# Retention followed by a squared-ReLU layer on one Trainium2 core: narrow idle matmuls, seven half-size products for one more block, and zeroing moved to GpSimd

## The chip, the cores and the metric

The kernel runs on one core of a Trainium2 chip. The metric is the device time of one execution in microseconds (us). Three runs of the kernel before took 204.18, 204.24 and 204.94 us; their median is 204.24 us. Engines are named as in the profile: PE is the matmul engine (PEld its weight load), DVE the vector engine, ACT the scalar engine, POOL is GpSimd, SP issues most DMAs.

## The reference, cut to what matters

```python
# q, k, v: (B=4, H=8, S=768, D=64) float32; w_in (512, 2048), w_out (2048, 512)
gamma = 1.0 - 2.0 ** (-5.0 - np.arange(H))
for t in range(S):
    state = gamma[None, :, None, None] * state + einsum('bhd,bhe->bhde', k[:, :, t], v[:, :, t])
    y[:, :, t] = einsum('bhd,bhde->bhe', q[:, :, t], state) / sqrt(D)
x = y.transpose(0, 2, 1, 3).reshape(B * S, H * D)      # 3072 tokens x 512
h = maximum(x @ w_in, 0)
out = (h * h) @ w_out                                   # 3072 x 512, float32
```

A recurrent attention ("retention") with a fixed decay for each head gives 512 numbers per token; a feed-forward layer of width 2048 with a squared ReLU follows.

## The kernel before, in words

**Tiling.** The 3072 tokens are 24 chunks of 128. The chunks are grouped in 11 blocks (`BLOCKS`, L18): block 0 has four chunks, blocks 1 to 10 have two each. For each chunk the retention is computed in its chunked form: scale q and k by powers of the decay (DVE, L361, L697), transpose them (PE, or a DMA transpose from chunk 8 on), scores (PE, L430 or L727), mask (DVE, L437 or L734), running state (PE, L458, L469 or L754, copied out to `s_bd`), outputs (PE, L498/L506 or L776/L783, copied to `xt` by ACT). For each block the layer follows: **first products** `x @ w_in` (PE, L826) into a PSUM tile, ReLU by ACT (L835), square on DVE (L806) or, for some tiles, on ACT (L804); then **second products** with `w_out`.

**Two forms of the second products.** The plain form (L1152) takes, for a chunk of 128 tokens, 16 matmuls of 128x512; a block of two chunks needs 32. In the other form (`seven_products`, L840) the product of a 2x2 partition of h (two chunks by even and odd 128-row slices) with a 2x2 partition of `w_out` is made by seven products of half the width instead of eight: 7 x 8 matmuls of 128x256 (L860), with sums of h tiles made ahead on DVE (`s1` to `s4`, L856), sums of weight tiles made once (`sum_w_out`, L319) and the results put together by DVE adds (`u`, `v`, `osb`). `SEVEN` (L28) says which blocks use it: 2 to 10. Its last product is kept (`kept`) and issued between the next block's first products. Blocks up to 2 issue their first products in units of 16 matmuls of 128x128 (`first_unit`), one for each quarter g and chunk c; later blocks in tiles of 128x512. Block 0 (`last_of_first`, L959) makes chunks 0 and 1 plainly (L1017) and chunks 2 and 3 by seven products (L984).

**What sets the order.** All instructions are issued in an order written by hand, one queue per engine, each in order; waits are semaphores. The layer's work is cut in pieces (8 for a chunk, numbered from the start), and `put(n, what, ...)` hangs attention work, loads, casts and zeroing behind piece n. `attend` (L1258) places the unpacked attention of chunks 4 to 7, `attend2` that of chunks 8 to 23. Work hung behind one piece is issued in the order in which it was put. Squares are issued at the next piece, after what is hung there.

**Buffers that matter here.** PSUM: `tp`, `st`, `y` and `c_ps` have one buffer each, `psf` four. A tile that takes a buffer waits until the last reader of the tile before it is done. `st` holds scores until DVE has masked them; `tp` holds transposes, and from block 2 on also the product `pa` of `seven_products`. In SBUF `h2` has three buffers of 128x4096 bf16, taken in turn; the first is `spare` (L1180), which lends room to block 0's `s1`, `s2`, `s4`. From block 2 on these sums lie in `k_bds` and `v_bds[0]`, which the attention of chunks 0 to 7 no longer needs.

**The start.** While q, k and v are loaded, `keep_awake` (L337) issues matmuls whose results nobody reads: 15 of 128x512, with the identity matrix as both operands, which POOL builds first.

**Zeroing.** Five tiles need zeros off their diagonal before chunk 8: `zero_off_diagonal` (L357) does it by ten DVE memsets behind pieces 35 to 44. `pack_constants` (L261) builds the decay table and the mask for chunks 8 and later; its POOL part hangs behind piece 27, its DVE and ACT part behind piece 34.

The pieces of block 0 are 5 to 32, of block 1 33 to 48. The wait in block 0 that the change touches lies in these lines: the ACT copy reads `pa`, and the next matmuls add to `pa`.

```python
nc.scalar.activation(a[:], pa, AF.Copy)          # L1041
...
product(pa, a12, b(1, 0), lo, False)             # L1047
product(pa, a12, b(1, 0), hi, False)
```

Of the kernel before, what the change touches and what calls it, by code (L numbers as in the profile page):

```python
# [9 lines left out]
FP32 = mybir.dt.float32  # L10
BF16 = mybir.dt.bfloat16
# [13 lines left out]
PACK_FROM = 8  # L25


SEVEN = range(2, 11)  # L28


@with_exitstack
def kernel(
# [148 lines left out]
        load_w_in(g)  # L181


    lng = const.tile([P, H], FP32)
    for h in range(H):
        nc.gpsimd.memset(lng[:, h : h + 1], float(np.log(gammas[h])))
# [147 lines left out]

    idle_ps = []

    def keep_awake(n, width=4 * C, pool=ps_f, name="psf"):  # L337
        if not idle_ps:
            idle_ps.append(pool.tile([P, 4, P], FP32, name=name))
        wide = max(1, width // C)  # L340
        for _ in range(n):
            nc.tensor.matmul(
                idle_ps[0][:, 0:wide, 0 : width // wide],
                lhsT=ident[:],
                rhs=ident[:, None, 0 : width // wide].to_broadcast([P, wide, width // wide]),
                start=True,
                stop=True,
            )

    def end_awake():  # L350
        idle_ps.clear()
# [3 lines left out]
    xts = {}  # L355

    def zero_off_diagonal(t, hh):  # L357
        nc.vector.memset(t[halves[hh], :, 1 - hh, :], 0.0)

    def scale(engine, out, by, table):  # L360
        engine.tensor_tensor(  # L361
# [478 lines left out]
    def seven_products(tb):  # L840
# [4 lines left out]
            t.rearrange("s p hh d -> s (p hh d)").rearrange("s (j t) -> s j t", t=C)  # L845
            for t in (k_bds[0], k_bds[1], v_bds[0])
        )
        s3 = a21
        t1, t2, t3, t4 = sums
        b11, b21, b22 = (  # L850
# [108 lines left out]
    def last_of_first():  # L959
# [43 lines left out]
        def second_products():  # L1003
            ops = [ps_f.tile([P, DM], FP32, name="psf") for _ in range(2)]
            pa, pe, pd, pb = (
                t[:, n * HN : (n + 1) * HN]
                for t in [ps_f.tile([P, DM], FP32, name="psf") for _ in range(2)]
                for n in range(2)
            )
            oa, ob = (opool.tile([P, DM], FP32, name="osb") for _ in range(2))  # L1010
            a, u, v = (upool.tile([P, HN], FP32, name=f"u{i}") for i in range(3))
            r0 = 2 * C

            def plain(j):
                for f in (2 * j, 2 * j + 1):
                    for c, op in enumerate(ops):
                        nc.tensor.matmul(  # L1017
                            op[:],
                            lhsT=h_of(0, f)[:, 0, c * C : (c + 1) * C],
                            rhs=w_out_bf[f // FPQ][:, f % FPQ, :],  # L1020
                            start=(f == 0),
                            stop=(f == NFB - 1),
                        )
                product(pa, a11, b(0, 0), (j,))

            lo, hi = range(0, 4), range(4, 8)
            for j in range(4):
                plain(j)
                yield
            product(pd, s1, t1, lo)  # L1030
            product(pb, s2, t2, lo, False)
            yield
            for j in range(4, 6):
                plain(j)
                yield
            product(pe, a22, t4, lo, False)
            yield
            plain(6)
            yield
            plain(7)  # L1040
            nc.scalar.activation(a[:], pa, AF.Copy)  # L1041
            for c, op in enumerate(ops):
                osb = opool.tile([P, DM], FP32, name="osb")
                nc.scalar.activation(osb[:], op[:], AF.Copy)
                nc.sync.dma_start(out[c * C : (c + 1) * C], osb[:])
            yield
            product(pa, a12, b(1, 0), lo, False)  # L1047
            product(pa, a12, b(1, 0), hi, False)
            nc.scalar.activation(oa[:, 0:HN], pa, AF.Copy)
            yield  # L1050
            product(pd, s1, t1, hi)
            yield
            product(pb, s2, t2, hi)
            add(u[:], pb, a[:])
            yield
            product(pe, a22, t4, hi)
            yield
            product(pb, s3, t3, lo, False)
            yield
            product(pb, s3, t3, hi, False)  # L1060
            add(v[:], pb, a[:])
            add(ob[:, HN:DM], pd, v[:])
            add(ob[:, 0:HN], pe, v[:])

            def last_product():
                product(pd, s4, b(1, 1), range(8), False)
                add(oa[:, HN:DM], pd, u[:])
                yield
                nc.sync.dma_start(out[r0 + C : r0 + 2 * C], ob[:])
                yield  # L1070
                nc.sync.dma_start(out[r0 : r0 + C], oa[:])
                yield

            kept.append(last_product())
            yield
# [5 lines left out]
    def first_unit(tb, g, c, parts=(0, 1)):  # L1081

        if tb not in h2s:
            h_tiles(tb)
        if (tb, g, c) not in open_ps:
            open_ps[tb, g, c] = ps_f.tile([P, FPQ, C], FP32, name="psf")
        hp = open_ps[tb, g, c]
        cols = slice(c * C, (c + 1) * C)
        half = FPQ // 2
        for part in parts:  # L1090
            for fq in range(part * half, (part + 1) * half):
                first_product(tb, hp[:, fq, :], g * FPQ + fq, cols)
        if 1 in parts:
            relu(h_of(tb, g * FPQ, (g + 1) * FPQ)[:, :, cols], open_ps.pop((tb, g, c)))

    def ffn_pieces(tb):
        nch = BLOCKS[tb]
# [29 lines left out]
        else:  # L1127
# [4 lines left out]
            for f0 in range(0, NFB, per):  # L1132
                hp = ps_f.tile([P, per, TB], FP32, name="psf")
                for f in range(f0, f0 + per):
                    first_product(tb, hp[:, f - f0, :], f, slice(0, TB))
                relu(h_of(tb, f0, f0 + per), hp, tb in SEVEN and f0 // per in (1, 3))
                if f0 // per in (1, 2, 3) and kept:
                    next(kept[0])
                if f0 // per == 4:
                    kept.clear()  # L1140
                if f0 // per == 5 and tb in SEVEN:
                    first_sums(slice(0, 4))
                yield
# [33 lines left out]
    def small_pt():  # L1177
        return ptpool.tile([P, NPAIR, 2, C], BF16, name="pt").rearrange("s p hh t -> s (p hh t)")

    spare = hpool.tile([P, 4096], BF16, name="h2")  # L1180
    keep_awake(7, pool=ps_y, name="y")
    scale_q4(0, 0)
    scale_q4(0, 1)
    transpose_q4(0, 0, *tp)
# [73 lines left out]
    def attend(m, scaled, places):  # L1258
        if m % 2 == 0:
            put(scaled, scale_q, m, 0)  # L1260
            put(scaled + 2 if m == 4 else scaled, scale_q, m, 1)
            put(places[0], transpose_q, m)
        put(18 if m == 4 else places[0], scale_kv, m)
        put(places[1], transpose_k, m)
        put(places[2], scores, m, 0)
        put(places[3], scores, m, 1)
        put(places[3], state, m)
        put(places[4], outputs, m)

    def attend2(m, d, before, q_at, qturn_at, k_at, turn_at, v_at):  # L1270
# [24 lines left out]
            put(place, next, made)  # L1295
    attend(4, 13, (19, 21, 23, 25, 29))
    attend(5, None, (25, 28, 30, 32, 34))
    attend(6, 31, (33, 35, 37, 39, 42))
    attend(7, None, (38, 42, 44, 46, 49))
    packed = pack_constants()  # L1300
    put(27, next, packed)
    put(34, next, packed)
    for j, t in enumerate([s_bds[2]] + ks_bd2s + v_bd2s):
        for hh in range(2):
            put(35 + 2 * j + hh, zero_off_diagonal, t, hh)
# [68 lines left out]
```

## Time and profile before

The profile is of one execution, which took 204.98 us; from its first to its last instruction it took 203.1 us.

| | |
|---|---|
| median of three runs | 204.24 us |
| profiled execution, its own time | 204.98 us |
| its span | 203.1 us |
| PE busy | 195.3 us (96%), 2351 matmuls |
| DVE busy | 154.7 us (76%) |
| ACT busy | 127.5 us (63%) |
| POOL busy | 67.5 us (33%) |

"Busy" counts from an instruction's start to its modelled end; the matmuls of one engine overlap, so how long a row of them takes is read from the start of one group to the start of the next. A bracket in a timeline, such as [1.06 <-ACT h L835], says how long the engine had been idle and which instruction's end let it go on. `x8` means that eight equal instructions are merged in one line.

### The profile page before, as it was taken

How to read it: one execution, taken by the hardware profiler on the slowest of the kernel's cores; microseconds unless marked ns; L12 is line 12 of the kernel's file. 1: busy time of each engine (PE TensorE's matmuls, PEld its weight loads, DVE VectorE, ACT ScalarE, POOL GpSimd, SP SyncE). 2: the span in 40 equal slices, each digit the busy share in tenths (PEclk: the TensorE clock that was granted, in tenths of full speed). 3: DMA queues.
4: the chain of work that ended last, by engine and by line, in shares of the span. 5: the costliest groups of instructions: out<-in, count | busy, mean ns of one | idle time of the engine just before them, and what ended most of it. 6: DMA issues, size and time to landing. Idle time of an engine off the chain costs nothing.

```text
span 203.1 us, 5810 instructions
## 1 busy us (share of the span) xinstructions
PE 195.3 (96%) x2351; PEld 162.2 (80%) x2351; DVE 154.7 (76%) x322; ACT 127.5 (63%) x258; POOL 67.5 (33%) x131
## 2 busy tenths in 40 slices
PE   5799999999999999999999999999999999999993
PEld 1368545679965998988989999999989899999883
DVE  3886798888798678788798798798797797485374
ACT  8774873365743766782794784784785775763730
POOL 8594630261300451372234325252225225100000
PEclk9999999999999999999999999999999999999999
DMA  5999999999869898989787978968899342200202
GB/s 171 353 371 398 317 192 196 249 233 263 245 164 197 213 169 141 218 221 237 148 223 137 255 219 201 255 137 208 223 151 211 114 103 58 103 3 0 107 0 103
DMA packets 92250, 38.12 MB, mean 188 GB/s; under 512 B 68544, under 2 KB 88256, under 8 KB 92224
## 3 DMA queue, kind: packets, MB, share of 16 engines
q1 hardware_dynamic: 90112, 35.66, 72.4%
q0 software_dynamic: 2112, 2.10, 6.4%
q8 instruction: 18, 0.29, 0.6%
q14 instruction: 8, 0.07, 0.1%
HBM read 27.26 MB, written 6.29 MB: 165 GB/s over the span
## 4 chain that ended last, share of the span: by engine, by line
PE 88%; DVE 4%; DMA 3%; ACT 2%; SPq 1%; issue 1%; DVEq 0%
PE psf L826 40%; PE psf L860 18%; PE tp L860 7%; PE psf L1017 3%; PE psf L1152 3%; DMA kn<-in_k_dram 3%; PE psf L984 3%; PE y L783 2%; PE st L727 2%; PE y L776 2%; PE c_ps L754 2%; DVE h L806 1%; PE c_ps L627 1%; PE y L506 1%; PE st L430 1%
## 5 line engine op out<-in xcount | busy, mean ns | idle before, releaser
L826 PE MATMUL psf<-xt,w_in_bf 128*128 128x256 bf16 (+2 forms) x880 | 92.3, 259 | 0.4 <-issue 0.4
L826 PEld LDWEIGHTS <-w_in_bf 128*128 128x128 bf16 x880 | 71.2, 98 | 11.6 <-issue 0.4
L835 ACT ACTIVATE h<-psf 128x512 bf16<-128x512 f32 x96 | 56.1, 595 | 21.5 <-PE psf L826 20.0
L806 DVE TENSOR_TENSOR h<-h 128x512 bf16<-128x512 bf16 x80 | 35.3, 455 | 18.4 <-ACT h L835 18.2
L688 POOL CAST ks_bdp<-stage 64x512 bf16<-64x512 f32 x32 | 22.7, 711 | 38.4 <-issue 34.1
L705 POOL COPY v_bd<-v 64x512 bf16<-64x512 bf16 x32 | 20.5, 642 | 44.4 <-DVE v L697 33.6
L860 PEld LDWEIGHTS <-h 128*128 128x128 bf16 x288 | 26.3, 98 | 3.6 <-DVE h L806 0.7
L860 PE MATMUL tp<-w_out_bf,h 128*128 128x256 bf16 x136 | 19.4, 273 | 0.2 <-DVE h L806 0.2
L860 PE MATMUL psf<-w_sum,h 128*128 128x256 bf16 x136 | 19.1, 273 | 0.0
L860 PE MATMUL psf<-w_sum,k_bd 128*128 128x256 bf16 x144 | 17.9, 273 | 0.0
L361 DVE TENSOR_TENSOR qs<-qn,qf 128x512 bf16<-128x512 f32 x20 | 16.2, 814 | 0.0
L860 PEld LDWEIGHTS <-k_bd 128*128 128x128 bf16 x144 | 13.7, 98 | 1.5
L856 DVE TENSOR_TENSOR osb<-psf,u 128x256 f32<-128x256 f32 x26 | 10.3, 420 | 6.1 <-PE psf L860 5.8
L763 ACT ACTIVATE s_bd<-c_ps 64x256 bf16<-64x256 f32 x29 | 10.7, 370 | 6.3 <-PE c_ps L754 6.3
L856 DVE TENSOR_TENSOR u<-psf,u 128x256 f32<-128x256 f32 x18 | 7.6, 422 | 9.3 <-PE psf L860 9.1
L697 DVE TENSOR_TENSOR v<-stage,kf 128x512 bf16<-128x512 f32 x16 | 12.1, 759 | 0.0
L734 DVE TENSOR_TENSOR pt<-st,cmask 128x512 bf16<-128x512 f32 x16 | 11.0, 687 | 0.3 <-issue 0.2
L764 ACT ACTIVATE s_bd<-c_ps 64x256 bf16<-64x256 f32 x29 | 11.0, 378 | 0.4
L856 DVE TENSOR_TENSOR k_bd<-h 128x512 bf16<-128x512 bf16 x18 | 10.7, 596 | 0.3
L790 ACT ACTIVATE xt<-y 128x512 bf16<-128x512 f32 x16 | 9.6, 598 | 1.8 <-PE y L783 1.2
L896 ACT ACTIVATE osb<-tp 128x256 f32<-128x256 f32 x8 | 3.1, 384 | 12.2 <-PE tp L860 12.2
L804 ACT ACTIVATE h<-h 128x512 bf16<-128x512 bf16 x16 | 10.1, 629 | 0.5
(145 smaller groups left out, 283.8 us busy)
## 6 DMA issues: line engine op xcount, KB each, us to landing
qn<-in_q_dram SPq DMA_DIRECT2D x12, 512.0 KB, 5.2
out_dram<-osb SPq DMA_DIRECT2D x23, 256.0 KB, 2.7
stage<-in_k_dram SPq DMA_DIRECT2D x32, 96.0 KB, 3.8
stage<-in_v_dram SPq DMA_DIRECT2D x32, 96.0 KB, 3.5
stage<-in_moe_w_in_dram SPq DMA_DIRECT2D x4, 512.0 KB, 7.2
stage<-in_moe_w_in_dram SPq DMA_DIRECT2D x2, 1024.0 KB, 10.3
w_out_bf<-in_moe_w_out_dram POOLq DMA_DIRECT2D x4, 512.0 KB, 10.2
kn<-in_k_dram SPq DMA_DIRECT2D x6, 256.0 KB, 6.3
```

What stands on the lines that cost most here:

```text
L361: engine.tensor_tensor(out=out, in0=by, in1=table[:, :, None].to_broadcast([P, H, D]), op=ALU.mult)
L688: nc.gpsimd.tensor_copy(ks[rows, :, hh, :].rearrange("s (u p) d -> s u p d", u=2), kn[rows])
L697: nc.vector.tensor_tensor(out=v2.rearrange("s (u p) d -> s u p d", u=2), in0=vn, in1=kf2[:, i, :, :, None].to_broadcast([P, 2, NPAIR, D]), ...
L705: nc.gpsimd.tensor_copy(v_bd[rows, :, hh, :], v2[rows])
L734: nc.vector.tensor_tensor(out=pt[:], in0=st[:], in1=cmask2.rearrange("s r t -> s (r t)")[:, None, :].to_broadcast([P, 2 * NPAIR, C // 2]), ...
L763: nc.scalar.activation(s_bd[halves[0], :, 0, :], c[halves[0]], AF.Copy)
L764: nc.scalar.activation(s_bd[halves[1], :, 1, :], c[halves[1]], AF.Copy)
L806: nc.vector.tensor_mul(hv, hv, hv)
L826: nc.tensor.matmul(hp, lhsT=w_in_bf[g][:, cb, fq * 128 : (fq + 1) * 128], rhs=xts[tb][:, cb, cols], start=(cb == 0), stop=(cb == NCB - 1),)
L835: nc.scalar.activation(hv, hp[:], AF.Relu)
L856: nc.vector.tensor_tensor(out=out, in0=in0, in1=in1, op=op)
L860: nc.tensor.matmul(to, lhsT=left[:, j], rhs=right(j) if callable(right) else right[:, j], start=(start and j == 0), stop=(stop and j == NF ...
```

## The change

- `keep_awake`: each idle matmul of 128x512 becomes four of 128x128. Operands are 128 columns of zeros at the end of `spare`, set by a DVE memset that is now DVE's first instruction, instead of the identity; the first batch is 10 x 4 instead of 7.
- Block 0, after the plain products: the second halves of the products `pd` and `pb` now come before the two halves of `pa += a12 * b`, which they followed.
- Block 1 joins `SEVEN`: 56 matmuls of 128x256 take the place of 32 of 128x512. Its `s1`, `s2`, `s4` lie in a further `h2` buffer (`room`), since `k_bds` and `v_bds` are still in use. One of its squares, that of unit (1, 2), goes to ACT.
- The transposed k of chunk 7 goes through `st` instead of `tp`, since `pa` of block 1 now holds `tp`.
- Both copies of chunk 6's state go to ACT; the second half of q of chunk 6 is scaled two pieces after the first, and both earlier (29, 31 instead of 31, 31); chunk 7's steps come one or two pieces earlier.
- `pack_constants` moves from pieces 27 and 34 to 18 and 22.
- The ten zeroing memsets go to POOL.
- Block 4 gets one more square on ACT (tile 6).

```diff
-SEVEN = range(2, 11)
+SEVEN = range(1, 11)
...
+    spare = hpool.tile([P, 4096], BF16, name="h2")
+    still = spare[:, 4096 - P : 4096]
+    nc.vector.memset(still, 0.0)
...
-    def keep_awake(n, width=4 * C, pool=ps_f, name="psf"):
+    def keep_awake(n, pool=ps_f, name="psf"):
...
+        for _ in range(4 * n):
+            nc.tensor.matmul(idle_ps[0][:], lhsT=still, rhs=still, start=True, stop=True)
...
     def zero_off_diagonal(t, hh):
-        nc.vector.memset(t[halves[hh], :, 1 - hh, :], 0.0)
+        nc.gpsimd.memset(t[halves[hh], :, 1 - hh, :], 0.0)
...
+        if tb == 1:
+            room = hpool.tile([P, 4096], BF16, name="h2").rearrange("e (n j t) -> e n j t", n=4, t=C)
+            s1, s2, s4 = (room[:, n] for n in range(3))
...
+            product(pd, s1, t1, hi)
+            product(pb, s2, t2, hi)
+            add(u[:], pb, a[:])
+            yield
             product(pa, a12, b(1, 0), lo, False)
+            yield
             product(pa, a12, b(1, 0), hi, False)
             nc.scalar.activation(oa[:, 0:HN], pa, AF.Copy)
-            yield
-            product(pd, s1, t1, hi)
-            yield
-            product(pb, s2, t2, hi)
-            add(u[:], pb, a[:])
             yield
...
-            relu(h_of(tb, g * FPQ, (g + 1) * FPQ)[:, :, cols], open_ps.pop((tb, g, c)))
+            relu(h_of(tb, g * FPQ, (g + 1) * FPQ)[:, :, cols], open_ps.pop((tb, g, c)), (tb, c, g) == (1, 1, 2))
...
-                relu(h_of(tb, f0, f0 + per), hp, tb in SEVEN and f0 // per in (1, 3))
+                relu(h_of(tb, f0, f0 + per), hp, tb in SEVEN and f0 // per in ((1, 3, 6) if tb == 4 else (1, 3)))
...
-    spare = hpool.tile([P, 4096], BF16, name="h2")
-    keep_awake(7, pool=ps_y, name="y")
+    keep_awake(10, pool=ps_y, name="y")
...
-            put(scaled + 2 if m == 4 else scaled, scale_q, m, 1)
+            put(scaled + 2, scale_q, m, 1)
...
-        put(places[1], transpose_k, m)
+        put(places[1], transpose_k, m, *((ps_st, "st") if m == 7 else (ps_tp, "tp")))
...
-        put(places[3], state, m)
+        put(places[3], state, m, 2 if m == 6 else 1)
...
-    attend(6, 31, (33, 35, 37, 39, 42))
-    attend(7, None, (38, 42, 44, 46, 49))
+    attend(6, 29, (33, 35, 37, 39, 42))
+    attend(7, None, (36, 40, 43, 45, 48))
     packed = pack_constants()
-    put(27, next, packed)
-    put(34, next, packed)
+    put(18, next, packed)
+    put(22, next, packed)
```

More of the change, by code (lines that the diff above doesn't have):

```diff
@@ L335 @@
     idle_ps = []
-    def keep_awake(n, width=4 * C, pool=ps_f, name="psf"):
+    def keep_awake(n, pool=ps_f, name="psf"):
         if not idle_ps:
[L339 to L348, printed above, removed]
+            idle_ps.append(pool.tile([P, P], FP32, name=name))
+        for _ in range(4 * n):
+            nc.tensor.matmul(idle_ps[0][:], lhsT=still, rhs=still, start=True, stop=True)
     def end_awake():
```

## The prediction, as it was put on record

> **What bounds the kernel.** First the page: the busy shares, then the 40 slices.
>
> ```profile
> PE 195.3 (96%) x2351; PEld 162.2 (80%) x2351; DVE 154.7 (76%) x322; ACT 127.5 (63%) x258; POOL 67.5 (33%) x131
> ...
> PE   5799999999999999999999999999999999999993
> ...
> PE 88%; DVE 4%; DMA 3%; ACT 2%; SPq 1%; issue 1%; DVEq 0%
> ```
>
> PE is full from the third slice (about 10 us) to the last; the chain that ended last is 88% PE. So a matmul taken out between 12 and 195 us shortens the kernel, and so does a PE wait that goes; work on DVE, ACT or POOL counts only where PE waits for it. I therefore looked in the timelines for starts of PE groups later than the matmuls before them allow.
>
> The first place is the end of block 0's plain products. Columns: start, duration, engine, line, operation, count, idle time and its releaser.
>
> ```profile
> 42.20 0.27 PE L984 MATMUL psf<-w_out_bf,h 128*128 128x256 bf16 x1
> 42.95 1.03 PE L984 MATMUL psf<-w_out_bf,h 128*128 128x256 bf16 x8 [0.47 <-ACT u L1041]
> ```
>
> A 256-column matmul occupies PE for 0.11 us (eight of L860 start at 76.98, the next group at 77.85), so PE was free at 42.31 and stood until 42.95: **0.64 us** for ACT's copy of `pa`.
>
> The second is block 1's second product, and what comes just before it.
>
> ```profile
> 56.09 0.39 PE L430 MATMUL st<-qT,k_bd 128*128 128x128 bf16 x4
> 56.41 0.32 PE L469 MATMUL c_ps<-v_bd,ks 128*64 128x64 bf16 x8
> 56.66 1.07 PE L826 MATMUL psf<-xt,w_in_bf 128*128 128x128 bf16 x16
> 57.56 1.89 PE L1152 MATMUL psf<-w_out_bf,h 128*128 128x512 bf16 x8
> 59.29 0.77 PE L506 MATMUL y<-pt,v_bd 128*128 128x128 bf16 x8
> ```
>
> Eight L1152 take 59.29 - 57.56 = 1.73 us.
>
> The third is DVE in the same stretch; spacings between starts are what I use below.
>
> ```profile
> 54.62 0.42 DVE L806 TENSOR_TENSOR h<-h 128x512 bf16<-128x512 bf16 x1 [1.06 <-ACT h L835]
> 54.96 0.68 DVE L437 TENSOR_TENSOR pt<-st,cmask 128x512 bf16<-128x512 f32 x1
> 55.64 0.27 DVE L358 MEMSET ks_bdp<- 64x256 uint32 x1
> 55.83 0.84 DVE L361 TENSOR_TENSOR qs<-qn,qf 128x512 bf16<-128x512 f32 x1
> 56.60 0.41 DVE L806 TENSOR_TENSOR h<-h 128x512 bf16<-128x512 bf16 x1
> 56.94 0.68 DVE L361 TENSOR_TENSOR ks<-kn,kf 128x512 bf16<-128x512 f32 x1
> 57.70 0.27 DVE L358 MEMSET ks_bdp<- 64x256 uint32 x1
> 57.99 0.69 DVE L361 TENSOR_TENSOR qs<-qn,qf 128x512 bf16<-128x512 f32 x1
> 58.60 0.42 DVE L806 TENSOR_TENSOR h<-h 128x512 bf16<-128x512 bf16 x1
> 58.93 0.69 DVE L437 TENSOR_TENSOR pt<-st,cmask 128x512 bf16<-128x512 f32 x1
> ```
>
> The mask of chunk 6's second half of scores (`pt`, 58.93) ends at 59.62, 3.3 us after its scores: DVE is behind, and in the kernel before nobody on PE asks for it until 61.84.
>
> **The change part by part.**
>
> *Wait in block 0: -0.64.* At 42.31 PE now has 8 matmuls of `pd` and `pb`, 0.87 us, ready; ACT's copy (42.51 to 42.89) ends beneath them. Their weight sums `t1`, `t2` are done by 41.5 (42.1 if shifted as in the next step).
>
> *What is late next there: +0.2.* `pack_constants` puts a cast and a multiply on DVE ahead of block 0's last sums. They need POOL's iotas, which follow the v cast (35.78, 1.10 long) by 1.0 us (41.93 lng, 42.40 iota, 0.58 long): ready at 37.9, where DVE was free at 37.4. Cast and multiply take 0.5 to 0.8 (51.24 to 52.01 before), so the sums move by 1.1 to 1.4; 0.74 of that is DVE's idle time before the mask at 39.50. What is left, 0.3 to 0.6, moves k of chunk 5 (42.61, ends 43.30) to 43.6-43.9 and `t4`'s second half (ends 44.54) to 44.9-45.1. PE, now earlier, wants them at 43.62 (42.31 + 12 x 0.109) and 44.95. I take 0.2; bounds 0 and 0.35. Without the move nothing would be late.
>
> *Second product of block 1: -0.83.* Out: 4 x 1.73 = 6.92 us. In: 7 x 0.87 = 6.09 us.
>
> *What is late next there: +0.66.* The transposes of chunk 7's k now write `st`, right behind the last unit of first products. `st` is free when DVE has masked chunk 6's second scores, the last DVE line above. PE is 0.64 - 0.2 = 0.44 us earlier, so the unit ends at 57.56 - 0.44 = 57.12. DVE's stretch starts with a square that waited for ACT, whose ReLU follows PE, so it moves with PE: 54.62 - 0.44 = 54.18. Then, by spacings and without memsets and with `ks` moved ahead into the 1.06 us of idle time: square 0.34, mask 0.61, q 0.61, square 0.34, q 0.61, square 0.34, and the mask's 0.69: 54.18 + 3.54 = 57.72, and some 0.06 to PE (`pt` 46.44 + 0.69, PE on at 47.19). So PE stands from 57.12 to 57.78: 0.66. Everything behind waits: k copies on ACT, all seven products. Bounds 0 (DVE 0.66 faster) and the 1.6 of the slower rival.
>
> *DVE and ACT for the seven products: 0.* The sums needed first (`s1`, `s2`, 57.7 to 59.7 with the square of unit (1,3) between, each 0.42) are wanted by PE at 60.3; that square needs ReLU at 57.9 to 58.4 (ACT first does two state copies 0.38 and the square 0.63) and ends at 58.9, wanted at 57.78 + 0.22 + 14 x 0.109 = 59.5. Cover is 0.6 us in both; if it is gone, the stall grows one for one. `u`, `v` and `osb` (0.42 each) are ordered as in block 2, where PE does not wait for them. Their stores join SP's queue in block 2 in place of the two L1164 stores; the next DMA transposes do not move.
>
> *Memsets on POOL: 0.* Ten of 0.52 (L298 memsets 64x512) from about 51 to 57, where POOL was idle but for two casts; the casts of chunk 8's k behind them end at 58 instead of 56.1, and SP takes that tile at 65.81. DVE is relieved by 10 x 0.19 to 0.29, counted above where it bears.
>
> *Idle matmuls: 0.* PE starts at about 1.0 (one memset) instead of 2.18. The old ones start 0.43 us apart at first, 0.107 for 128 columns: 40 take 4.3, done by 5.3, before the first transposes at 5.53. The chain runs through the landing of k at 9.6; after it three batches of four lie on the path, 4 x 0.055 (four 128-column transposes L404 take 0.22) against 0.215. Upper bound +0.5, if each cost the 98 ns of a weight load; lower bound 0, because 9.6 does not move.
>
> *The 162 more PE instructions* (57 idle, 24 product matmuls, each with a load): the chain has one piece "issue" of 0.39 at 17.34 that no semaphore explains. Another like it: +0.4; its going: -0.4; I take 0.
>
> *Block 4's square on ACT: 0.* PE has no gap there. Block 3 has one: L860 waits until 92.16 for an L806 square, about 0.5 us in all with one at 90.40. DVE runs there beside four POOL casts (88.56 to 91.8), and nothing of that order changes, so I keep it. Bounds -0.5 and +0.2.
>
> **Sum:** -0.64 + 0.2 - 0.83 + 0.66 = **-0.6 us**. The profiled execution took 204.98, span 203.1 and 1.9 around it; it lies 0.74 above the median. Like against like it would become 204.4, and the median 204.24 becomes **203.6 us**.
>
> **The rivals.**
>
> *DVE is in time.* If DVE frees `st` by 57.1, the 0.66 goes: -1.27, 203.0 us; with block 3's wait gone too, -1.8, 202.4. For it: only 0.66 us of DVE work must be elsewhere, and memsets and `ks` have left. Against it: the count above has already taken them out, and each row in it is measured.
>
> *POOL's memsets slow DVE* (slower than before). Beside POOL's casts the same DVE operations with two SBUF inputs are longer: the L856 sums 0.82 at 88.69 and 0.72 at 89.55 against 0.42, three squares 1.91 at 90.19 against 0.42 each. If memsets do this, the mask that frees `st` comes 3 x 0.2 + 2 x 0.16 = 0.9 later (stall 1.6), the first sums and the square (0.4 + 0.3 + 0.2 later) hold PE 0.4 more, the second pair 0.7: stalls 2.7 in place of 0.66, in all +1.4, 205.7 us. It turns slower than before once DVE loses over 0.6 us. Against it: at 4.79 two L533 multiplies beside POOL's memsets took 1.29 us, and at 7.29 with POOL idle 1.29. Those are f32, not the bf16 squares. The Trainium skill (GPSIMD Engine Reference, section 8, Key points) says that GpSimd shares its SBUF interfaces with VectorE and that VectorE instructions with two SBUF inputs contend; by that rule this rival would be the outcome. The trace agrees for casts (0.82 against 0.42), not for the memsets beside L533.
>
> *The change does not do what it says:* the saved PE time is all lost again to DVE, as if both late steps reached their bounds (0.35 and 1.1): 0 to +0.3, 204.2 to 204.6.
>
> **How the numbers follow.** Forecast 0.45 (its own range 203.1 to 204.1), DVE in time 0.32, all lost again 0.12, slower by memsets 0.11. The range leaves out the last and the lowest tail: 202.4 to 204.8. About 0.5% (1.0 us) is what a measurement of this kernel can tell from no change. Faster than 203.2 is the rival of DVE in time and a tenth of the forecast: 0.36. Slower than 205.3: 0.10. The rest, 0.54, is within.
>
> **What would show it.** In the new profile: the L984 wait for `u` L1041 gone; the PE line of k transposes into `st` waiting some 0.6 us for DVE's `pt`; from the end of the last unit to block 2's L754 0.8 us less without that wait; squares beside POOL memsets at 0.42, not 0.62; a short PE wait for `ks` near 43.7. I am wrong if PE goes through the `st` transposes without a gap, if DVE's rows in block 1 are not those of before, or if PE's first 20 us move.

## The result, and the profile after

The changed kernel took **205.75 us** (median of six runs, 205.45 to 206.25), the kernel before, in the same session, 204.38 us (six runs, 204.18 to 204.94). The ratio is 1.0065, 95% interval 1.0048 to 1.0081: slower by 1.3 us, where 203.6 had been forecast, with a range of 202.4 to 204.8. The profiled execution took 206.25 us, with a span of 204.5 us (before: 204.98 and 203.1).

The answering lines of its page: busy shares, PE's slices, and the chain that ended last.

```profile
PE 196.8 (96%) x2432; PEld 169.1 (83%) x2432; DVE 156.9 (77%) x321; ACT 128.6 (63%) x261; POOL 72.2 (35%) x141
...
PE   8999999989989999999999899999999999999993
...
PE 75%; DVE 7%; DMA 6%; issue 3%; SPq 3%; ACT 3%; POOL 1%; DVEq 0%
```

PE is still the fullest engine, but its share of the chain fell from 88% to 75%. The busy shares hide this; the chain does not. DVE's share of the chain rose from 4% to 7%, that of DMA from 3% to 6%, that of SP's queue from 1% to 3%, and three of PE's slices (the ninth, twelfth and twenty-third, which start at some 41, 56 and 112 us) are no longer full. The waits of PE name the new links. (Lines of attention and layer code stand three lower than before: L401 was L404, L427 was L430, L724 was L727, L803 was L806, L823 was L826. L984, L1017 and L1041 are where they were.) Columns: engine, line, releaser, total us, times, longest.

```profile
...
PE st L401 <- DVE pt L434: 0.9, 1, 0.9
PE psf L984 <- ACT osb L1054: 0.6, 1, 0.6
PE st L724 <- DMA kT<-ks_bdp: 0.6, 1, 0.6
...
PE tp L401 <- DVE ks L358: 0.2, 1, 0.2
```

The list counts idle time of the modelled matmuls. Below I give losses by starts: the spacing to the next group, less what the matmuls before it take. The wait of L984 for `u` L1041 (0.64) is gone, as forecast; four others have come.

**Block 0.** PE after the plain products:

```profile
41.78 1.04 PE L984 MATMUL psf<-w_sum,h 128*128 128x256 bf16 x8
42.66 0.60 PE L984 MATMUL psf<-w_out_bf,h 128*128 128x256 bf16 x4
43.43 0.40 PE L401 MATMUL tp<-ident,ks 128*128 128x128 bf16 x4 [0.17 <-DVE ks L358]
43.66 0.60 PE L984 MATMUL psf<-w_out_bf,h 128*128 128x256 bf16 x4
...
44.66 0.28 PE L503 MATMUL y<-pt,v_bd 128*128 128x128 bf16 x2
45.52 0.60 PE L984 MATMUL psf<-w_sum,h 128*128 128x256 bf16 x4 [0.58 <-ACT osb L1054]
```

and ACT in the same stretch:

```profile
41.98 0.39 ACT L1041 ACTIVATE u<-psf 128x256 f32<-128x256 f32 x1 [0.60 <-PE psf L984]
42.27 1.08 ACT L1044 ACTIVATE osb<-psf 128x512 f32<-128x512 f32 x2
43.86 1.20 ACT L408 ACTIVATE k_bd<-tp 64x512 bf16<-64x512 bf16 x2 [0.52 <-PE tp L401]
45.08 0.39 ACT L1054 ACTIVATE osb<-psf 128x256 f32<-128x256 f32 x1
```

ACT's copy of `pa` runs beneath PE's eight matmuls at 41.78. Then PE waits 0.33 us for k of chunk 5 (the four matmuls at 42.66 are through at 43.10, at 0.109 us each; the transposes start at 43.43), and 0.75 us before the second half of `pe` (45.52). That half needs ACT's copy `oa` (L1054), because `pa` and `pe` are the two halves of one `psf` tile: a write to one waits for the reader of the other. The new order puts the end of a piece, and with it the transposes of chunk 5, between the two halves of `pa += a12 * b`, so on ACT the two k copies (L408, 1.20) stand ahead of `oa`.

**Block 1.** PE, and DVE beside it:

```profile
56.59 1.07 PE L823 MATMUL psf<-xt,w_in_bf 128*128 128x128 bf16 x16
58.52 0.38 PE L401 MATMUL st<-ident,ks 128*128 128x128 bf16 x4 [0.86 <-DVE pt L434]
58.74 0.82 PE L860 MATMUL tp<-w_out_bf,h 128*128 128x256 bf16 x6
```

```profile
54.55 0.43 DVE L803 TENSOR_TENSOR h<-h 128x512 bf16<-128x512 bf16 x1 [0.68 <-ACT h L832]
54.90 0.68 DVE L434 TENSOR_TENSOR pt<-st,cmask 128x512 bf16<-128x512 f32 x1
55.50 0.68 DVE L358 TENSOR_TENSOR qs<-qn,qf 128x512 bf16<-128x512 f32 x1
56.10 0.42 DVE L803 TENSOR_TENSOR h<-h 128x512 bf16<-128x512 bf16 x1
56.43 0.68 DVE L358 TENSOR_TENSOR qs<-qn,qf 128x512 bf16<-128x512 f32 x1
57.03 0.83 DVE L803 TENSOR_TENSOR h<-h 128x512 bf16<-128x512 bf16 x1
57.79 0.68 DVE L434 TENSOR_TENSOR pt<-st,cmask 128x512 bf16<-128x512 f32 x1
```

PE is done at 57.50 (sixteen matmuls from 56.59) and stands until 58.52, 1.02 us, for the mask that frees `st`. It is the chain of the prediction, in its order, with one link of another length: the third square took 0.83 instead of 0.42. POOL shows why:

```profile
54.65 2.19 POOL L355 MEMSET v_bd<- 64x512 bf16 x4
56.89 1.45 POOL L685 CAST ks_bdp<-stage 64x512 bf16<-64x512 f32 x2
```

The squares at 54.55 and 56.10 ran beside memsets and were not held up; the one at 57.03 met the cast of chunk 8's k.

**Later.** Block 2 waits 0.18 us for a square (at 76.7), and at 113.29 the scores of chunk 14 start 0.73 us late, for the DMA transpose `kT`. SP's queue in the kernel before, then after:

```profile
105.19 1.95 SPq L145 DMA_DIRECT2D stage<-in_v_dram  x3
107.24 1.71 SPq L711 DMA_TRANSPOSE kT<-ks_bdp  x1
```

```profile
106.40 1.94 SPq L145 DMA_DIRECT2D stage<-in_v_dram  x3
108.45 1.27 SPq L708 DMA_TRANSPOSE kT<-ks_bdp  x1
```

SP issues this transpose 1.2 us later, and it lands at 113.24 instead of 110.88. Three loads of v stand right before it, 0.65 us each to issue; the last of them took 4.59 us from its issue to its landing, and 3.45 in the kernel before. The later issue alone does not make PE wait: in another execution of the kernel before (before_again, below) SP came to the transpose later still, and PE had no wait there.

```profile
108.73 1.28 SPq L711 DMA_TRANSPOSE kT<-ks_bdp  x1
```

**The account.** Starts of the same groups on PE in the two profiled executions, after less before: -0.53 at the scores of chunk 4 in block 0 (41 us), -0.07 behind block 0 (46), 0.00 behind block 1 (70), +0.26 behind block 2 (82), +1.00 from 112 on. Another 0.4 lies behind the last matmul, at the kernel's end. The first -0.53 comes from loads: k landed at 8.94 us here and at 9.58 before, with the same loads in the same order, of which 0.34 is left at 39 us; and at 39.92 the kernel before waits for a load of `w_out` that landed at 39.88, which is on time here (39.19). Whether the change has a part in that stays open (the experiments come back to it).

### The profile page after: what moved, and what is told of

It reads as the page before. It is cut to its first block, busy times and chain, and to the rows that moved or that the text cites. A ratio compares the mean times of both kernels' runs of the same rounds, so it can differ in the third digit from the quotient of the medians.

```text
span 204.5 us, 5986 instructions
## 1 busy us (share of the span) xinstructions
PE 196.8 (96%) x2432; PEld 169.1 (83%) x2432; DVE 156.9 (77%) x321; ACT 128.6 (63%) x261; POOL 72.2 (35%) x141
## 4 chain that ended last, share of the span: by engine, by line
PE 75%; DVE 7%; DMA 6%; issue 3%; SPq 3%; ACT 3%; POOL 1%; DVEq 0%
PE psf L823 36%; PE psf L860 18%; PE tp L860 7%; DMA vn<-in_v_dram 4%; PE psf L1017 3%; DMA kT<-ks_bdp 2%; DVE h L803 2%; PE psf L984 2%; PE st L724 2%; SPq L115 2%; PE y L780 2%; DVE w_sum L323 2%; PE y L773 1%; PE c_ps L751 1%; ACT h L832 1%
## 5 line engine op out<-in xcount | busy, mean ns | idle before, releaser
L823 PE MATMUL psf<-xt,w_in_bf 128*128 128x256 bf16 (+2 forms) x880 | 92.3, 259 | 0.0
L823 PEld LDWEIGHTS <-w_in_bf 128*128 128x128 bf16 x880 | 71.2, 98 | 11.0
L803 DVE TENSOR_TENSOR h<-h 128x512 bf16<-128x512 bf16 x78 | 35.6, 471 | 17.3 <-ACT h L832 16.9
L685 POOL CAST ks_bdp<-stage 64x512 bf16<-64x512 f32 x32 | 23.3, 729 | 36.4 <-issue 27.3
L860 PEld LDWEIGHTS <-h 128*128 128x128 bf16 x344 | 31.5, 98 | 4.3 <-DVE h L803 1.0
L860 PE MATMUL psf<-w_sum,h 128*128 128x256 bf16 x168 | 23.4, 273 | 0.0
L860 PE MATMUL tp<-w_out_bf,h 128*128 128x256 bf16 x152 | 21.9, 273 | 0.2 <-DVE h L803 0.2
L860 PE MATMUL psf<-w_sum,k_bd 128*128 128x256 bf16 x144 | 17.9, 273 | 0.0
L856 DVE TENSOR_TENSOR osb<-psf,u 128x256 f32<-128x256 f32 x29 | 11.5, 422 | 6.7 <-PE psf L860 6.3
L856 DVE TENSOR_TENSOR u<-psf,u 128x256 f32<-128x256 f32 x20 | 8.4, 422 | 9.1 <-PE psf L860 9.0
L860 PEld LDWEIGHTS <-k_bd 128*128 128x128 bf16 x144 | 13.7, 98 | 1.5
L801 ACT ACTIVATE h<-h 128x512 bf16<-128x512 bf16 x18 | 11.4, 631 | 0.6
```

Source lines behind the costliest of these rows:

```text
L685: nc.gpsimd.tensor_copy(ks[rows, :, hh, :].rearrange("s (u p) d -> s u p d", u=2), kn[rows])
L801: nc.scalar.activation(hv, hv, AF.Square)
L803: nc.vector.tensor_mul(hv, hv, hv)
L823: nc.tensor.matmul(hp, lhsT=w_in_bf[g][:, cb, fq * 128 : (fq + 1) * 128], rhs=xts[tb][:, cb, cols], start=(cb == 0), stop=(cb == NCB - 1),)
L856: nc.vector.tensor_tensor(out=out, in0=in0, in1=in1, op=op)
L860: nc.tensor.matmul(to, lhsT=left[:, j], rhs=right(j) if callable(right) else right[:, j], start=(start and j == 0), stop=(stop and j == NF ...
```

## The experiments

The theory from these rows: the forecast gains are real, but each brought PE early to something that another engine's order or a shared buffer sets: (a) `oa` behind the k copies, (b) `st` behind DVE's mask, (c) SP's queue, that is, the DMAs issued ahead of the transpose. Rivals: the memsets on POOL, the idle matmuls, or the half-size products themselves cost the time. Ratios below are to the kernel before, run beside it; medians of the kernel before were 204.88, 204.57 and 204.63 us in the three sessions. The changed kernel's own ratio, 1.0065, is from the first comparison; a ratio has an interval of some 0.002 to each side, so what one edit brings, as the difference of two ratios, is known to some 0.5 us, and the profiles must say what became of each wait.

**oa_first: both halves of `pa += a12 * b` again in one piece**, so that ACT copies `oa` ahead of the k copies.

```diff
             product(pa, a12, b(1, 0), lo, False)
-            yield
             product(pa, a12, b(1, 0), hi, False)
             nc.scalar.activation(oa[:, 0:HN], pa, AF.Copy)
             yield
+            yield
             product(pe, a22, t4, hi)
```

> The changed kernel with one edit: in block 0 both halves of pa += a12 * b and ACT's copy of pa are issued in one piece, so that the copy stands ahead of the copies of chunk 5's k on ACT. Theory (new PE waits): pe shares a PSUM tile with pa, so its second half waits for ACT's copy of pa, which stood behind two k copies (0.75 us), and the k transposes asked for DVE's k 0.33 us too early; both go, and 0.15 us for the k copies comes: 0.9 us faster than the changed kernel, 204.8 or 0.4 above the kernel before. Rival (the memsets on POOL slow DVE): no change from 205.7, since DVE's rows stay as they are. The wait of PE for the st buffer in block 1 stays at 0.9 to 1.0 under both.

Measured: 205.35 us, 1.0034 [1.0016, 1.0051]. ACT and PE of this run:

```profile
44.00 0.38 ACT L1053 ACTIVATE osb<-psf 128x256 f32<-128x256 f32 x1 [0.39 <-PE psf L984]
44.28 1.20 ACT L408 ACTIVATE k_bd<-tp 64x512 bf16<-64x512 bf16 x2
```

```profile
44.58 0.28 PE L503 MATMUL y<-pt,v_bd 128*128 128x128 bf16 x2
44.81 0.61 PE L984 MATMUL psf<-w_sum,h 128*128 128x256 bf16 x4
```

The 0.75 is gone, so (a) is shown: the edit moves the second half of `pa` and with it `oa`, and nothing else. (The 0.33 for k is gone too, since that half, four matmuls, now stands ahead of the transposes.) It gives back 0.6 us (1.0065 less 1.0034) where 0.9 was expected, because smaller waits come up there instead (0.12, 0.21 and 0.15 in the profile).

**k7_psf: the transposes of chunk 7's k through `psf`, which has four buffers, instead of `st`.**

```diff
-        put(places[1], transpose_k, m, *((ps_st, "st") if m == 7 else (ps_tp, "tp")))
+        put(places[1], transpose_k, m, *((ps_f, "psf") if m == 7 else (ps_tp, "tp")))
```

> The changed kernel with one edit: the transposed k of chunk 7 takes one of the four psf buffers instead of st. Theory (new PE waits): PE's 1.02 us before the transposes goes; 0.35 us comes back at the square of unit (1, 3), which DVE ends at 59.6 and PE now wants at 59.2: 0.65 us faster than the changed kernel, 205.1. Rival (the memsets on POOL slow DVE): DVE is as late as before, the wait moves to the first sums whole: no change from 205.7.

Measured: 205.14 us, 1.0031 [1.0016, 1.0046].

```profile
57.50 0.39 PE L401 MATMUL psf<-ident,ks 128*128 128x128 bf16 x4
57.72 0.82 PE L860 MATMUL tp<-w_out_bf,h 128*128 128x256 bf16 x6
58.38 0.82 PE L860 MATMUL psf<-w_sum,h 128*128 128x256 bf16 x6
59.03 0.38 PE L860 MATMUL tp<-w_out_bf,h 128*128 128x256 bf16 x2
59.65 0.39 PE L860 MATMUL psf<-w_sum,h 128*128 128x256 bf16 x2 [0.24 <-DVE h L803]
```

The transposes start at 57.50, the moment PE is free: (b) is shown. Of the 1.02 us, 0.40 comes back at 59.65, where the products reach the square of unit (1, 3), the next thing DVE is late with. The prediction had counted 0.6 us of cover there; without the wait for `st` PE is 1.0 us earlier and uses it up.

**memset_dve: the ten memsets back on DVE.**

```diff
-        nc.gpsimd.memset(t[halves[hh], :, 1 - hh, :], 0.0)
+        nc.vector.memset(t[halves[hh], :, 1 - hh, :], 0.0)
```

> The changed kernel with one edit: the ten zeroing memsets go back to DVE. Theory (new PE waits): the square that ran beside POOL's cast of chunk 8's k (0.83 us at 57.03) takes 0.42 again, since that cast comes at 52 to 56 as before, but two or three memsets of 0.2 to 0.3 us stand in DVE's queue ahead of the mask that frees st: the wait for st 0.9 to 1.2 us, the time 205.6 to 205.9. Rival (the memsets on POOL slow DVE and so make the whole loss): 204.3 or less.

Measured: 205.97 us, 1.0078 [1.0054, 1.0103] (four runs; the interval overlaps that of the changed kernel). PE at `st`:

```profile
58.94 0.38 PE L401 MATMUL st<-ident,ks 128*128 128x128 bf16 x4 [1.12 <-DVE pt L434]
```

With memsets on DVE the wait grows from 1.02 to 1.28 us, and from 46 to 82 us PE loses 0.90 us against the kernel before, where the changed kernel loses 0.33. So the rival falls: on POOL the memsets do not slow DVE, and the squares beside them at 0.42 said so already. It was the casts that held a square up. Two things hide this in the time: this profile has no wait for `kT` of chunk 14, and the 0.4 us at the kernel's end are gone in it. This run differs from the changed kernel in the memsets alone, so those 0.4 us come with their move to POOL.

**three_fixes: `oa_first` and `k7_psf`, with POOL's memsets two by two behind pieces 30 to 34** instead of one behind each of the pieces 35 to 44, so that the cast of chunk 8's k might come earlier.

```diff
-            put(35 + 2 * j + hh, zero_off_diagonal, t, hh)
+            put(30 + j, zero_off_diagonal, t, hh)
```

> The changed kernel with three edits: oa_first, k7_psf, and the ten memsets on POOL behind pieces 30 to 34 instead of 35 to 44, so that POOL does them in its idle time before the v cast of chunk 7 and the cast of chunk 8's k comes back to 52 to 56 us. Theory (new PE waits): 0.9 for the first; with the square at 0.42 again DVE ends the square of unit (1, 3) before PE wants it, so the whole 1.0 of the second: 1.9 us faster than the changed kernel, 203.8, which is 0.6 faster than the kernel before. Rival (seven products in block 1 bring nothing here, because DVE's sums hold PE back wherever they stand): 204.8, that is oa_first alone.

Measured: 204.65 us, 1.0000 [0.9973, 1.0027]: the whole loss is back, and none of the gain. Some 0.4 us of it is the kernel's end, where the additional time is gone. In the profile PE is 1.07 us ahead of before at 107 us and 0.38 at 112: scores of chunk 14 wait 0.69 us for `kT`. Here SP is not late:

```profile
107.31 1.27 SPq L708 DMA_TRANSPOSE kT<-ks_bdp  x1
```

That is when the kernel before issues it (107.24), but the load of v ahead of it took 4.38 us and not 3.45, and the transpose lands 1.0 us later (111.88). So most of what PE saves in blocks 0 and 1 it loses again to a late landing. The early memsets did not part cast and square: the second cast waits for its load, which lands at 55.5, and still meets a DVE operation.

**four_spread: `three_fixes`, and the loads of v of that group spread out**, so that two of them are issued behind the transpose and not ahead of it.

```diff
-[58, 59, 60, 61, 62, 64, 65, 66] + [82 + j for j in range(8)]
+[58, 59, 60, 61, 62, 64, 65, 66] + [82 + 3 * j // 2 for j in range(8)]
```

> three_fixes and one edit: of the second half of the loads of v for chunks 15 to 17, two move behind the DMA transpose of chunk 14's k in SP's queue (places 82 + 3j//2 instead of 82 + j). Theory (SP's queue is the next limit): in the profile of three_fixes PE waits 0.69 us at 111 for that transpose, which lands 1.0 us later than in the kernel before although SP issues it at the same time, behind a load that landed as late; two loads of 0.62 us less ahead of it bring it 1.2 us ahead: the wait goes, 0.7 us less, ratio to the kernel before 0.9965. Rival (the 0.69 is a floor of the DMA traffic as a whole): the wait stays within 0.2, ratio 1.000.

Measured: 204.42 us, 0.9990 [0.9968, 1.0011]. In the profile SP issues the transpose at 105.24 and it lands at 109.18; the scores no longer wait:

```profile
110.40 1.04 PE L823 MATMUL psf<-xt,w_in_bf 128*128 128x256 bf16 x8
111.27 0.40 PE L724 MATMUL st<-qT,kT 128*128 128x64 bf16 x8
```

PE keeps its 1.03 us to the end, and this execution has a span of 202.1. So (c) holds in the trace in this form: with two loads fewer ahead of the transpose, which makes its issue 2.1 us earlier than in three_fixes, the wait is gone. In the median the gain (0.2 us) is smaller than the interval.

**five_sq3: `four_spread`, and the additional square on ACT in block 3 instead of block 4.**

```diff
-relu(h_of(tb, f0, f0 + per), hp, tb in SEVEN and f0 // per in ((1, 3, 6) if tb == 4 else (1, 3)))
+relu(h_of(tb, f0, f0 + per), hp, tb in SEVEN and f0 // per in ((1, 3, 6) if tb == 3 else (1, 3)))
```

> four_spread and one edit: the third square on ACT is that of block 3 instead of block 4. Theory (block 3's 0.54 us of waiting comes from three DVE squares of 0.6 us beside POOL casts): with one of them on ACT 0.35 us less, ratio 0.9945; and block 4 shows no wait without its square on ACT, as in the kernel before. Rival (ACT's ReLUs become late instead): no change from four_spread.

Measured: 203.97 us, 0.9971 [0.9953, 0.9989]: faster than before by 0.6 us. Of block 3's 0.54 (0.15 and 0.38) the 0.38 is gone. The same profile shows 0.40 at 126.35 for another `kT`, that of a later transpose: the wait moves on.

**wide_idle: the old idle matmuls in the changed kernel** (7 x 1 of 128x512 on the identity, no zeros in `spare`).

```diff
-    still = spare[:, 4096 - P : 4096]
-    nc.vector.memset(still, 0.0)
...
-        for _ in range(4 * n):
-            nc.tensor.matmul(idle_ps[0][:], lhsT=still, rhs=still, start=True, stop=True)
+        for _ in range(n):
+            nc.tensor.matmul(idle_ps[0][:, 0:4, 0:C], lhsT=ident[:],
+                rhs=ident[:, None, 0:C].to_broadcast([P, 4, C]), start=True, stop=True)
```

> The changed kernel with the old idle matmuls: 128x512 from the identity, seven first. Theory (new PE waits): the idle matmuls are off the path, no change from the changed kernel, ratio 1.0065 within 0.0015. Rival (narrow idle matmuls, with a weight load each, cost time at the start): 0.5 us less, ratio 1.004.

Measured: 205.88 us, 1.0057 [1.0031, 1.0083], the changed kernel's own ratio within the interval. The rival's 1.004 lies in it too, so the medians do not decide. The profile speaks for the forecast: at 41 us PE is 0.46 us ahead of the kernel before, where the changed kernel is 0.53 and 0.52 ahead in its two profiles. It has the waits of 0.75 and 1.02, and none for k of chunk 5 or for `kT`.

**noseven: the changed kernel without the seven products in block 1** (`SEVEN` from 2 again, chunk 7's k through `tp`).

```diff
-SEVEN = range(1, 11)
+SEVEN = range(2, 11)
...
-        put(places[1], transpose_k, m, *((ps_st, "st") if m == 7 else (ps_tp, "tp")))
+        put(places[1], transpose_k, m)
```

> The changed kernel with block 1's second product by 32 matmuls of 128x512 again, and chunk 7's k transposed through tp again; all else as changed. Theory (new PE waits): back come 0.83 us of matmuls, away go 1.02 at st, 0.2 at block 2's first square and 0.1 behind it: 0.5 us less, ratio 1.004; what is left is block 0's. Rival (the seven products gain their 0.83 and the loss is all in block 0): ratio 1.0105.

Measured: 205.12 us, 1.0026 [1.0006, 1.0046], 0.8 us faster than the changed kernel. So block 1's seven products, 0.83 us less PE work, were a net loss as put in. In its profile PE is 0.53 us ahead behind block 1 (70 us), 0.16 more than ahead of it (0.37), where the changed kernel lost 0.07 there; and the waits of block 2 and for `kT` are missing. With `st` mended and the loads spread they are worth having: in four_spread PE gains 0.54 between 56 and 70 us (0.65 to 1.19 ahead).

**before_again and after_again: both kernels unchanged**, one more profiled execution each, for how much a profile differs from itself.

> The kernel before once more, for its profile alone. In the changed kernel PE's first 12 us run 0.6 us ahead because the second and third loads land 0.6 earlier. Theory (that is the loads' own variation from execution to execution): of several executions of the kernel before, some have it too; if this one has, its span is 202.5 instead of 203.1. Rival (the idle matmuls' operand or start moves the loads): 203.1 again, with k landed at 9.6.

> The changed kernel once more, for its profile alone. Theory (new PE waits): the three waits of blocks 0 and 1 (0.33, 0.75, 1.02 us) stand again within 0.05, since they come from the order of the instructions; the wait for the transpose of chunk 14's k (0.73) varies, 0 to 0.8, since it hangs on when SP's queue comes to it. Rival (those waits are chance): they are not all there.

Measured: 204.93 and 205.78 us. In its second profile the changed kernel waits 0.75 and 1.02 again, and the 0.33 for k of chunk 5 is absent; `kT` costs 0.26 (chunk 10) instead of 0.73 (chunk 14), and a square in block 6 costs 0.33. So the two large waits belong to the kernel; the small ones, and where a transpose lands late, differ from one execution to the next. In this profile block 0 loses only 0.12 us against the kernel before (0.46 in the first), and the span is 0.8 to 0.9 us longer than those of the kernel before, not 1.4.

For `kT` of chunk 14 the second profile of the kernel before matters most. SP issues that transpose at 108.73, 1.5 us later than in the first and later than in either profile of the changed kernel (108.45, 108.17). It lands at 112.09, and PE, which wants it at 112.23, does not wait. So a queue that is 1.2 us late is nothing that only the change brings. Of the ten profiles with the loads of v in their old places, PE waits there (0.27 to 0.73 us) in four: the changed kernel's first, oa_first, k7_psf and three_fixes. They are the four in which the load right ahead of the transpose took longest, 4.38 to 4.60 us; in the other six it took 2.67 to 3.98.

The kernel before had k at 9.83 (9.58 the first time), the changed one at 9.07 (8.94). Of the other ten profiles, all of changed kernels, eight had it at 8.98 to 9.03, and oa_first and six_q31 at 9.80 and 9.69. wide_idle, with the old start, was early too, so the idle matmuls do not decide it. I did not find what does, nor whether the change has a part in it: both profiles of the kernel before are among the late ones.

**six_q31: `five_sq3` with chunk 6's q scaled as before** (both halves behind piece 31).

```diff
-            put(scaled + 2, scale_q, m, 1)
+            put(scaled + 2 if m == 4 else scaled, scale_q, m, 1)
...
-    attend(6, 29, (33, 35, 37, 39, 42))
+    attend(6, 31, (33, 35, 37, 39, 42))
```

> five_sq3 and one edit: q of chunk 6 is scaled in one go behind piece 31 as in the kernel before, so that the mask of chunk 5's first scores stands ahead of it on DVE. Theory (new PE waits): the mask starts at 45.4 to 45.6 instead of 45.91, st comes free 0.3 us earlier, and of PE's 0.2 us at 46.3 before the second scores 0.2 goes: ratio to the kernel before 0.996. Rival (what PE saves there it waits for elsewhere, k of chunk 5 above all): 0.997 as five_sq3.

Measured: 204.05 us, 0.9967 [0.9949, 0.9985]; no difference from five_sq3 that its interval shows. The 0.40 at the square of unit (1, 3) stays (0.41).

**five_oldorder: `five_sq3` with the old order of block 0's products**, with the 0.64 wait for `u` back.

```diff
-            product(pd, s1, t1, hi)
-            product(pb, s2, t2, hi)
-            add(u[:], pb, a[:])
-            yield
             product(pa, a12, b(1, 0), lo, False)
             product(pa, a12, b(1, 0), hi, False)
             nc.scalar.activation(oa[:, 0:HN], pa, AF.Copy)
             yield
-            yield
+            product(pd, s1, t1, hi)
+            yield
+            product(pb, s2, t2, hi)
+            add(u[:], pb, a[:])
+            yield
             product(pe, a22, t4, hi)
```

> five_sq3 with the order of block 0's products of the kernel before: pa first, then pd, then pb. Theory (new PE waits): the wait of 0.64 us for ACT's copy of pa comes back, and the 0.55 us of small waits that five_sq3 has in block 0 (0.21 before pe, 0.12 before the scores, 0.21 before the second scores) go but for 0.07: 0.16 slower, which these rounds can't tell from none, ratio 0.9975; its profile shows the one wait in place of the three. Rival (the new order is worth its 0.64): ratio 1.000.

Measured: 203.64 us, 0.9961 [0.9937, 0.9985], the fastest of all, 0.8 us faster than before. Its PE in block 0:

```profile
41.63 0.27 PE L984 MATMUL psf<-w_out_bf,h 128*128 128x256 bf16 x1
42.38 1.03 PE L984 MATMUL psf<-w_out_bf,h 128*128 128x256 bf16 x8 [0.47 <-ACT u L1041]
```

The old wait stands there in full, and behind it PE waits for nothing until 58.7: from 41 to 54 us it keeps its place against the kernel before (0.57 ahead at both). five_sq3, with the new order, goes from 0.41 to 0.55 ahead in that stretch and six_q31 from -0.06 to 0.22: of 0.64 removed, 0.14 to 0.28 stay, and the medians show none of it. The edit that looked safest in the prediction is the one that may be left out.

## Why the prediction was wrong, point by point

- **Wait in block 0, -0.64:** right. It is gone in every profile with the new order.
- **"What is late next there: +0.2": this step failed.** It looked at DVE only (k of chunk 5, `t4`) and put the bound at 0.35. The wait for k was 0.33 in one profile and nothing in the other, and where it came the cause was another: the cast and multiply of `pack_constants` (36.87 to 37.40) went into DVE's idle time, 0.42 us of which still stood before the mask at 39.16, and what made k late was a sum of weight tiles that met a cast on POOL (1.10 us instead of 0.69, last section). That the size fits is luck. What the step missed was ACT and a shared tile: `pe` and `pa` lie in one `psf` tile, and the new piece boundary put 1.20 us of k copies ahead of `oa`: 0.75 us. This wait stands in every profile of the order as changed, and goes with oa_first's one edit. Block 0 gave 0.46 us away by the account (-0.53 to -0.07; 0.12 in the second profile) where 0.44 of gain was forecast. Both facts stood in the code before: the four products are cut from two tiles, and an engine's queue is in order.
- **Second product of block 1, -0.83:** right in size; the L860 groups run at 0.109 a matmul (six in 0.65, at 58.74 and 59.39).
- **"What is late next there: +0.66":** mechanism right, size off. The chain was to take 3.54 us from its first square to the mask's end; from 54.55 that gives 58.09, and it ended some 0.4 later, all of it in the square beside the cast (0.83 for 0.42). PE and DVE were both some 0.38 later than forecast (57.50 for 57.12, 54.55 for 54.18), since block 0 had kept nothing, and that cancels. So 0.66 became 1.02. The prediction had both halves of this: it let the casts of chunk 8's k end at 58, and it listed DVE rows at 0.72 and 0.82 beside such casts. It did not lay one over the other.
- **DVE and ACT for the seven products, 0:** right as long as `st` holds PE up; without that, 0.40 (k7_psf), as the step's own condition said.
- **"The next DMA transposes do not move": the step left no room for what came.** In the first profile SP is 1.2 us late from block 2 to 112 us, where PE lost 0.73; in the second PE lost 0.26 at 82 us. The step counted the order of SP's queue and not its fill: in the kernel before SP spends 47.9 of the 52 us from 60 to 112 on issuing, which leaves little room to catch up. But the kernel before is as late in its second profile, and SP was on time in three_fixes, where PE waited. What goes with the waits at 112 us is how long the load ahead took to land, and what makes it long stays open.
- **Memsets on POOL, 0:** right for DVE, but the move brings 0.4 us at the kernel's end (memset_dve), which no step had. The rival built on them gave 205.7, almost the measured time, and is wrong all the same: DVE's squares beside memsets take 0.42, and with the memsets on DVE the kernel is no faster. By the Trainium skill (GPSIMD Engine Reference, section 8, Key points), DVE instructions with two SBUF inputs contend with GpSimd; the runs agree for casts (0.83) and not for memsets (0.42).
- **Idle matmuls, more PE instructions, block 4's square, 0:** nothing in the runs speaks against it, though no run tests the instructions alone. That block 3 was the place where a square on ACT is worth something stood in the prediction, which kept its wait as it was; five_sq3 takes 0.38 of it.
- **PE's first 20 us** moved by 0.6, named as a sign of being wrong; it goes with the landing of k, which varies from execution to execution.

From the forecast of -0.6: block 0 missed by 0.9, block 1 by 0.2, block 2's waits 0.25, `kT` 0.7, the kernel's end 0.4, against 0.5 of early loads: together +1.4, the difference of the two spans. The 0.4 at the end is in the closing semaphores behind the last store, where POOL stands 0.37 us between two of its own instead of 0.07. It is there in both profiles of the changed kernel and in oa_first, k7_psf, wide_idle and noseven, that is, wherever the memsets lie on POOL behind pieces 35 to 44, and absent with the memsets on DVE (the kernel before, memset_dve) or on POOL behind pieces 30 to 34 (three_fixes and all that build on it). So the edit that brings it is known; how it does so stays open.

## What to carry to other kernels

When PE is at 96%, taking a wait away moves PE onto the next order that is nearly late, so ask it of every queue (ACT's copies, DVE's chain, the DMAs ahead of a transpose) and of every buffer, halves of one tile included; the saving is what the second-latest leaves over. A chain of engine work that fits with less than 0.5 us to spare should be costed with one collision in it. A rival whose total matches the result is not thereby its cause: undo its one edit and see. And before a late DMA is put down to a change, a second profile of the kernel before shows how late it comes without it.

## What the runs showed of the hardware

Which of a POOL cast and a DVE operation with two SBUF inputs is held up went by which started first in the pairs seen here, and the later one lost most of the time that the earlier still needed. The same sum of weight tiles beside the same cast, in the two profiles of the changed kernel; first profile, DVE then POOL:

```profile
40.48 1.10 DVE L323 TENSOR_TENSOR w_sum<-w_out_bf,w_sum 128x1024 bf16<-128x1024 bf16 x1
```

```profile
40.43 0.61 POOL L374 CAST v_bd<-vn 128x512 bf16<-128x512 f32 x1 [3.09 <-DMA vn<-in_v_dram]
```

second profile:

```profile
40.48 0.69 DVE L323 TENSOR_TENSOR w_sum<-w_out_bf,w_sum 128x1024 bf16<-128x1024 bf16 x1
```

```profile
40.62 1.03 POOL L374 CAST v_bd<-vn 128x512 bf16<-128x512 f32 x1 [2.71 <-DMA vn<-in_v_dram]
```

The cast that started 0.05 us earlier, with 0.56 us still to run, cost DVE 0.41 us (and PE 0.33 behind it); started 0.14 later, when the sum had 0.55 to run, it lost 0.42 itself. In wide_idle the sum had 0.23 left when the cast started, and the cast lost 0.09 (0.70 instead of 0.61). A landing time 0.2 us apart decides it, and with it a wait on PE. Squares beside memsets on POOL took 0.42 to 0.43 us, as they do alone.

A DMA transpose landed after the load issued ahead of it, whenever that came: `kT` of chunk 14 landed 0.9 us after the last of three loads of v both before (110.88 and 109.96) and after (113.24 and 112.31), though that load took 3.45 us from its issue in the one and 4.59 in the other; over all 14 profiles it landed 0.90 to 1.91 us after the load ahead of it. So 1.2 us of delay in SP's queue became 2.4 at the landing.

What made the load longer is not shown by an experiment, but the traces have a trail. In the five profiles in which it took longest (3.98 to 4.60 us, after_again among them) a 16 KB packet of the instruction queue (q8 on the page) started 1.95 to 2.76 us after the load's issue, and the load landed 0.85 to 0.97 us after that packet's end. In memset_dve, wide_idle and noseven no such packet ran during the load, and it took 2.67 to 2.87 us. No run moves the packet alone, and elsewhere in these traces there are loads with such a packet beside them that land early, so this is a trail and no cause.
